# Attention with a mixture of experts on one core: the last bank's copy on VectorE in half of the turns, small gating work on GpSimd

## The chip, the core and the metric

The kernel runs on one core of a Trainium2 chip. A core has TensorE (in profile rows PE for matmuls and PEld for weight loads), VectorE (DVE), ScalarE (ACT), GpSimd (POOL), SyncE (SP), which issues DMAs, and 16 DMA engines. Matmuls write to PSUM, eight banks of 2 KB on each of 128 partitions; the other data lie in SBUF. The metric is the time of one execution in device microseconds (us).

## The reference

The inputs q, k and v are 8 batches x 8 heads x 576 positions x 64 values, in 32-bit floats. What is computed is attention with a block mask, and then a mixture of experts with a capacity of 80 tokens for each of 8 experts:

```python
scores = scale * np.matmul(q, k.transpose(0, 1, 3, 2))
mask = block_i >= block_j                      # blocks of 64 positions
scores = np.where(mask, scores, -1000000000.0)
scores = scores - np.max(scores, axis=-1, keepdims=True)
attn = np.exp(scores)
attn = attn / (np.sum(attn, axis=-1, keepdims=True) + 1e-09)
x = np.matmul(attn, v)                         # 4608 tokens x 512
logits = x @ w_gate
expert_idx = np.argmax(logits, axis=1)
gate_w = softmax(logits)[np.arange(N), expert_idx]
for e in range(8):                             # the 80 tokens of e with the largest gate_w
    out[tok_idx] = gate_w[tok_idx, None] * (np.maximum(x[tok_idx] @ w1[e], 0.0) @ w2[e])
```

## The kernel before, in words

**Pairs and turns.** A batch's eight heads are four pairs; pair i (0 to 31) belongs to batch i // 4. The loop at L799 runs one turn for each pair. Its order is written out by hand: the lists `TURN` (L40), `FIRST`, `LAST` (L139, the last turn, i = 31) hold steps as (distance, name, arguments), and turn i calls the step for pair i + distance. Every engine works through its own instructions strictly in this order and waits by semaphores.

**What a pair goes through.** `load` and `load_v` fetch q, k and v, five and three turns ahead; SP and GpSimd issue these DMAs. `prep` (L570) turns q (`prep 0`) and k (`prep 1`) on VectorE with one 128x576 transpose each; q is also scaled on GpSimd. `ends` and `scores` (TensorE) make the scores of the block-triangular tiles "08", "12", "34", "56" and "78", named after their blocks, 64 to 512 wide, into banks 2 to 7. `max` (VectorE) reduces a tile to its negated maximum; the tiles of the first and last block row are joined by `merge` (L635). `soft` (L640, ScalarE) takes the exponential of a tile with that maximum as bias, and accumulates its sum; the exponential of "78" needs `merge`. `sum "08"` (L648, VectorE) adds up tile "08". `back` (L653, TensorE) transposes the exponentials into banks A, B and C, two banks each (A0, A1 and so on), which `take` (L712) copies to SBUF: TAKE (L29) gives B0 to VectorE and the other five, and the results V0 and V1, to ScalarE. `values` (L683, TensorE) multiplies with v and needs all six copies. `flip` (VectorE) transposes the pair's result for the store.

**Where a turn stands in the trace.** Pair i's exponentials start at the end of turn i - 1. A "turn" in the tables below is the stretch from the first exponential of pair i to that of pair i + 1; it holds the bank copies of pair i, and so most of what turn i lists.

**The order around the change.** In `TURN`, VectorE has this order: small slots (below), max "56" head 0, copy B0, max "08" head 0, max "56" head 1, `prep 1` of pair i + 2, max "78" head 0, a small slot, max "08" head 1, max "78" head 1, `sum "08"`, `merge`, `prep 0`, the four reductions of "34" and "12", `flip`. ScalarE has: V1, V0, B1, A1, A0, C1, C0, then the ten exponentials.

**Gating in slots.** A batch's small work runs in slots: the step `t` (L769, seven in a turn, six of them ahead of max "56" and the seventh between max "78" head 0 and max "08" head 1; eleven in the last turn), `pe`, `ta`, and inside `values`. `enqueue` (L740) is called behind turn 4, 8, ..., 28, and puts generators into queues. In the queue `small` stand `recip` (L368: five little instructions and a reciprocal on VectorE, then the store on SP) and `products` (L420). In turn 5, 9, ... TensorE makes the batch's logits (`pe`), in turn 6, 10, ... it turns them (`logits2`) into banks 2 and 3, the banks of B; `products` reads them there. For batches 0 to 4 a queue in `slow` follows, in which GpSimd adds the products up in a tree and does part of the choice (`choose`, `index`, `total`, `turn`); for batches 5 to 7 `products` ends with a reduction on VectorE (L429), and `shift`, `first_of` and `weight` (L431 to L457) follow on VectorE in `small`. A slot runs one step of the first queue that has one ready; `HOLD_T` closes a queue until the next turn. Then `turn` on GpSimd spreads the weights, `turn2` on TensorE (inside `values`) sums them, and `placed` (VectorE) copies the result into Wt.

**The end.** Behind the last turn VectorE has, in this order, the flip of pair 30, the six instructions of the last batch's `recip`, and the copies of V1 and of a part of V0 (L826 to L839). The logits of batch 7, the choice of tokens, the fetch of the chosen rows, the experts' weights and the two matmuls of each expert follow.

In turn 1, `constants3` (L305) is issued ahead of the list: VectorE computes `cap` (L310) from `cf`, which GpSimd converts (L309).

Of the kernel before, what the change touches and what calls it, by code (L numbers as in the profile page):

```python
# [13 lines left out]
ALU = mybir.AluOpType  # L14
# [4 lines left out]
P = 128  # L19
BLK = 64  # L20
NT = 5
# [18 lines left out]
TURN = (  # L40
    (LEAD, "load"),
    (1, "begin"),
    (1, "ends"),
    (0, "t"),
    (0, "pe"),
    (0, "t"),
    (0, "t"),
    (0, "t"),
# [43 lines left out]
    (-1, "flip"),  # L92
    (3, "load_v"),
)

AHEAD = (
    (LEAD, "load"),
# [6 lines left out]
FIRST = (  # L104
    (LEAD, "load"),
    (1, "begin"),
    (2, "prep", 0),
    (1, "ends"),
    (1, "scores", "2"),
    (1, "max", "56", 0),  # L110
    (1, "soft", "56", 0),
    (1, "max", "56", 1),
# [26 lines left out]
LAST = (  # L139
    (0, "sum", "08"),  # L140
    (0, "pe"),
    (0, "back", "B"),
    (-1, "take", "V1", "v"),
    (-1, "take", "V0", "v"),
    (0, "back", "A"),
    (0, "take", "B0", "v"),
    (0, "take", "B1", "a"),
# [22 lines left out]
def tile_attn_moe(ctx, tc, q, k, v, w_gate, w1, w2, capacity, out, xs=None, dbg=None):  # L170
    nc = tc.nc
    B, H, S, D = q.shape
    NTOK, DM = out.shape
    E, _, F = w1.shape
    NP = H // 2
# [143 lines left out]
    def weights(n, after=None):  # L319
        for _ in loads(n, after):  # L320
            pass
# [33 lines left out]
    def banks(use, where=BANKS):  # L355
        return [psp[i].tile([P, 512], F32, name=f"bank{i}") for i in where[use]]

    class Batch:
# [7 lines left out]
            self.rs = sm.tile([P, NT, H], F32, name="rs", bufs=2)  # L366

        def recip(self):  # L368
            s_, s8 = self.sums, self.sums8
            yield nc.vector.tensor_tensor(s_[BLK:P, NT - 1], s_[BLK:P, NT - 1], s8[BLK:P], op=ALU.add)  # L370
            yield nc.vector.tensor_copy(s_[BLK:P, 0], s8[0:BLK])
            yield nc.vector.tensor_scalar(self.rs, s_, scalar1=1e-9, scalar2=None, op0=ALU.add)
            for to, of in ((slice(0, BLK), slice(BLK, P)), (slice(BLK, P), slice(0, BLK))):
                yield nc.vector.tensor_scalar(self.rs[to, 1], s_[of, 1], scalar1=1e-9, scalar2=None, op0=ALU.add)
            yield nc.vector.reciprocal(self.rs, self.rs)

        def flip(self, pr):

# [41 lines left out]
        def products(self):  # L420
            for pr in range(NP):
                iv = self.la[pr // 2][:, 0:BLK * NT].rearrange("p (t r c) -> p t r c", t=NT, r=2)[:, :, pr % 2, 0:2 * E]
                yield nc.vector.tensor_tensor(
                    prod[:, :, 2 * pr:2 * pr + 2], iv.rearrange("p t (s e) -> p t s e", s=2),
                    self.rs[:, :, 2 * pr:2 * pr + 2].unsqueeze(3).broadcast_to([P, NT, 2, E]), op=ALU.mult)
            if self.b < B - 3:
                return
            self.lg = sm.tile([P, NT, E], F32, name="lg", bufs=2)
            yield nc.vector.tensor_reduce(self.lg, prod.rearrange("p t h e -> p t e h"), axis=AX.X, op=ALU.add)  # L429
# [103 lines left out]
    HOLD_T = object()  # L533
# [182 lines left out]
    def warm(n, wt, after=None):  # L716

        if not n:
            return
        with ExitStack() as order:  # L720
            if after is not None:
                order.enter_context(tc.issue_after(after.ins))
            for i in range(n):
                nc.tensor.matmul(wt.rearrange("p (a c) -> p a c", c=P), lhsT=identr,
                                 rhs=identr.unsqueeze(1).broadcast_to([P, 4, P]), start=(i == 0), stop=(i == n - 1))

    n = B * NP
# [7 lines left out]
    wg_v = w_gate.rearrange("(r s d) e -> s d r e", s=2, d=D)  # L735
    cleared, kept = 0, 2

    pe_, small, slow, acts, turns, issued, held = [], [], [], [], [], {None}, []

    def enqueue(bt):  # L740

        def mark(tag):
            return lambda: issued.add((bt, tag))

        def fill(f, need=None, then=(), to=small):
            to.append((f(), need and (bt, need), then))

        pe_.extend(([bt.logits], [bt.logits2, mark("l2")]))
        turn_ = (lambda: bt.turn(nc.gpsimd), lambda: turns.append((bt, mark("t2"))))
        fill(bt.recip, None, (bt.store,))  # L750
        fill(bt.products, "l2", (mark("pr"),))
        if bt.b < B - 3:
            slow.append([])
            fill(bt.choose, "pr", (mark("sub"),), slow[-1])
            fill(bt.index, None, (), slow[-1])
            fill(bt.total, "ge", turn_, slow[-1])
            fill(bt.placed, "t2", (), slow[-1])
        else:
            fill(bt.shift, None, (mark("sub"),))
            fill(bt.first_of)  # L760
            fill(bt.weight, "ge", turn_)
            fill(bt.placed, "t2")
        acts.append((bt.expo, (bt, "sub"), mark("ge")))
# [3 lines left out]
            f()  # L767

    def t():  # L769
        for of in (small, *slow):  # L770
            while of and not any(of is x for x in held):
                g_, need, then = of[0]
                if need not in issued:
                    break
                step = next(g_, None)
                if step is HOLD_T:
                    held.append(of)
                if step is not None:
                    return
                of.pop(0)  # L780
                for f in then:
                    f()
# [13 lines left out]
    with tc.manual_schedule():  # L796
        warm(WARM[0], banks("g")[0])
        early = loads(FW0)
        for i in range(-LEAD, n):  # L799
            held.clear()  # L800
            if i == -1:
                nc.sync.dma_start(ci, capacity.bitcast(U32).partition_broadcast(P))
                for h in range(2):
                    nc.sync.dma_start(wgd[h * D:(h + 1) * D, :, h * E:(h + 1) * E], wg_v[h])

            for _ in range(min(4, nz - kept - cleared) if i >= n - 5 else 0):
                clear(cleared, nc.sync)
                cleared += 1
            if i == 1 - LEAD:
                nc.scalar.activation(early_exp, ramp[:, 2, 0:1], AF.Exp)  # L810
                constants()
            if i == -1:
                constants2()
            if i == 1:
                constants3()
            if i >= 2 and i % 3:
                next(early, None)
            for d, what, *args in FIRST if i == -1 else AHEAD if i == -2 else TURN if i < n - 1 else LAST:
                if what in slots_:
                    slots_[what]()  # L820
                elif 0 <= i + d < n and not (what == "flip" and n - NP <= i + d < n - 2):
                    getattr(pairs[i + d], what)(*args)
            if n - NP <= i + valued < n - 2:
                pairs[i + valued].flip()
            if i >= flipped and (i - flipped) % NP == NP - 1 and i - flipped < n - 1:
                enqueue(batches[(i - flipped) // NP])  # L826
        for _ in early:
            pass
        while not turns:
            t()  # L830
        bt = batches[B - 1]
        pairs[n - 2].flip()
        for _ in bt.recip():
            pass
        bt.store_sums()
        to, from_ = pairs[n - 1].out.pop("V0")
        pairs[n - 1].take("V1", "v")
        nc.scalar.copy(to[:, 0], from_[:, 0])
        nc.vector.tensor_copy(to[:, 1], from_[:, 1])  # L839
        att.close()  # L840
        fwa = late.enter_context(tc.tile_pool(name="fwa", bufs=FWA, **right, **tw))
        wpools += [fwa] * FWA
        lt = bt.logits_of()
        pairs[n - 1].flip()
        bt.store_x()
        weights(1)
        bt.logits_out(lt)
        bt.logits2()
        bt_, mark = turns.pop(0)
        bt_.turn2(banks("av")[0])  # L850
        mark()
        for _ in (*bt.products(), *bt.shift()):
            pass
        bt.expo()
        while small:
            t()
        found, weighed = bt.first_of(), bt.weight()
        for g_ in (found, found, found, weighed, found, weighed, weighed):
            next(g_)
        bt.turn(nc.vector, 2)  # L860
        bt.turn2(banks("L")[0])
        for _ in bt.placed():
            pass
# [92 lines left out]
    for i in range(NH):  # L956
        junk = sel2.tile([P, 2 * HC], BF16, name="junk", bufs=2)
        counted = vec.tensor_scalar(junk, pall[0][:, 0:2 * HC], scalar1=key[:, 0, i:i + 1], scalar2=None, op0=ALU.is_gt,
                          op1=ALU.add, accum_out=cnt_v[:, i:i + 1])
# [236 lines left out]
    with tc.If(again > 0):  # L1196
# [24 lines left out]
        step = 1.0  # L1221
# [32 lines left out]
        for i in range(2):  # L1254
# [4 lines left out]
                                   op0=ALU.mult, op1=ALU.add)  # L1259
# [29 lines left out]
        more = nc.values_load(nmore_i[0:1, 0:1], min_val=0, max_val=NPASS)  # L1289
# [93 lines left out]
```

## Time and profile before

| | us |
|---|---|
| median of 3 runs (lowest, highest) | 396.56 (396.32, 397.46) |
| the profiled execution | 393.76 |
| its span, first to last instruction | 392.0 |
| TensorE busy | 372.4 |
| ScalarE busy | 290.0 |
| VectorE busy | 279.8 |
| GpSimd busy | 185.4 |

The attention part takes the first 276 us or so of the span, the experts the rest. Times in rows are microseconds from the start of the span, unless marked ns. Busy times are unions over an engine's instructions; instructions of one engine overlap a little, so that the next can start before the one in front has ended. Matmuls are pipelined and their ends are modelled, so a TensorE that is always busy may still be waiting. In a timeline row stand start, length, engine, line, operation, what is written and read, and the count; in square brackets the idle time in front and what ended it.

### The profile page before, as it was taken

How to read it: one execution, taken by the hardware profiler on the slowest of the kernel's cores; microseconds unless marked ns; L12 is line 12 of the kernel's file. 1: busy time of each engine (PE TensorE's matmuls, PEld its weight loads, DVE VectorE, ACT ScalarE, POOL GpSimd, SP SyncE). 2: the span in 40 equal slices, each digit the busy share in tenths (PEclk: the TensorE clock that was granted, in tenths of full speed). 3: DMA queues.
4: the chain of work that ended last, by engine and by line, in shares of the span. 5: the costliest groups of instructions: out<-in, count | busy, mean ns of one | idle time of the engine just before them, and what ended most of it. 6: DMA issues, size and time to landing. Idle time of an engine off the chain costs nothing. (4 is left out here: it accounts for less than half of the span.)

```text
span 392.0 us, 15147 instructions
## 1 busy us (share of the span) xinstructions
PE 372.4 (95%) x5963; PEld 252.9 (65%) x5963; DVE 279.8 (71%) x787; ACT 290.0 (74%) x886; POOL 185.4 (47%) x383
## 2 busy tenths in 40 slices
PE   5899999999999999999999999998899899999991
PEld 3666667666766766766676676676578755665541
DVE  5879899999999989999999999899754230100010
ACT  1799999999999999999999999998122122323231
POOL 6246675566956867666696646500047010000010
PEclk9999999999999999999999999999999899999998
DMA  9989999999999999999999998998677999999801
GB/s 126 153 129 184 144 178 174 178 214 124 181 232 196 154 157 197 162 177 198 131 166 227 153 139 181 328 406 282 160 239 236 367 395 397 394 397 396 301 18 39
DMA packets 169916, 84.39 MB, mean 215 GB/s; under 512 B 132573, under 2 KB 151869, under 8 KB 169840
## 3 DMA queue, kind: packets, MB, share of 16 engines
q1 hardware_dynamic: 158352, 61.80, 74.5%
q0 software_dynamic: 9120, 21.27, 23.8%
q8 instruction: 49, 0.80, 1.0%
q10 hardware_dynamic: 2368, 0.30, 0.6%
q14 instruction: 27, 0.22, 0.2%
HBM read 63.21 MB, written 20.33 MB: 213 GB/s over the span
## 5 line engine op out<-in xcount | busy, mean ns | idle before, releaser
L644 ACT ACTIVATE P<-bank,negm 128x512 f32<-128x512 f32 (+3 forms) x320 | 158.2, 582 | 9.2 <-DVE negm L633 6.5
L597 PE MATMUL bank<-T,qt 64*128 64x320 f32 (+3 forms) x512 | 99.6, 498 | 0.6 <-DVE PT L714 0.6
L633 DVE TENSOR_REDUCE negm<-bank 128x1 f32<-128x320 f32 (+2 forms) x192 | 83.7, 474 | 11.0 <-PE bank L623 11.0
L696 PE MATMUL bank<-PT,vn 128*64 128x64 f32 (+3 forms) x1280 | 88.1, 293 | 0.6 <-ACT PT L714 0.6
L714 ACT COPY PT<-bank 128x512 f32<-128x512 f32 x158 | 81.8, 649 | 2.7 <-PE bank L678 2.2
L696 PEld LDWEIGHTS bank<-PT,vn 128*64 128x64 f32 x1280 | 56.3, 137 | 27.1 <-ACT PT L714 5.2
L580 POOL TENSOR_SCALAR qt<-T 128x128 f32<-128x128 f32 (+2 forms) x96 | 31.3, 344 | 87.5 <-DVE T L573 87.4
L644 ACT ACTIVATION_READ_ACCUMULATOR P<-bank,negm 128x1 f32 x256 | 70.0, 274 | 0.0
L678 PEld LDWEIGHTS bank<-ident,P 64*128 64x128 f32 (+1 forms) x1600 | 58.7, 137 | 12.2 <-issue 6.7
L678 PE MATMUL bank<-ident,P 64*128 64x64 f32 (+1 forms) x1600 | 64.5, 226 | 1.4 <-ACT P L644 0.6
L597 PEld LDWEIGHTS bank<-T,qt 64*128 64x128 f32 x512 | 48.1, 188 | 26.5 <-ACT PT L714 15.2
L633 DVE TENSOR_REDUCE raw<-bank 128x1 f32<-128x64 f32 (+1 forms) x128 | 51.7, 443 | 2.8 <-PE bank L597 1.9
L573 DVE STREAM_TRANSPOSE T<-ld 128x576 f32<-128x576 f32 x64 | 49.3, 771 | 2.7 <-DMA ld<-in_q_dram 1.5
L566 POOL DMA_DIRECT2D vn<-in_v_dram x58 | 46.0, 796 | 1.2 <-PE bank L702 0.8
L1164 POOL DMA_INDIRECT out_dram<-y,si x8 | 7.4, 928 | 74.3 <-DVE y L1159 74.3
L1102 PE MATMUL ps<-xsT,w 128*64 128x80 f32 x1024 | 39.9, 238 | 2.2 <-issue 1.7
L1159 DVE SCALAR_TENSOR_TENSOR y<-av,comb,yt 80x512 f32<-80x512 f32 (+1 forms) x8 | 5.6, 696 | 50.7 <-ACT yt L1158 49.9
L1102 PEld LDWEIGHTS ps<-xsT,w 128*64 128x64 f32 x1024 | 37.8, 140 | 5.8 <-issue 4.5
L558 POOL DMA_DIRECT2D ld<-in_k_dram x54 | 37.3, 697 | 3.8 <-DMA ld<-in_q_dram 3.5
L1155 PE MATMUL av<-w,hT 128*32 128x512 f32 (+2 forms) x320 | 39.0, 553 | 0.0
L1125 ACT ACTIVATE hT<-ps 128x320 f32<-128x320 f32 x16 | 7.0, 438 | 32.0 <-PE ps L1102 32.0
L1158 ACT ACTIVATE yt<-ps,gfar 32x512 f32<-32x512 f32 (+2 forms) x18 | 11.4, 636 | 24.7 <-PE ps L1155 24.6
(190 smaller groups left out, 436.5 us busy)
## 6 DMA issues: line engine op xcount, KB each, us to landing
w<-in_moe_w_dram SPq DMA_DIRECT2D x13, 2048.0 KB, 21.9
xs<-Y SPq DMA_DIRECT2D x32, 288.0 KB, 5.9
out_dram<-zero SPq DMA_DIRECT2D x18, 512.0 KB, 7.2
ld<-in_q_dram SPq DMA_DIRECT2D x126, 72.0 KB, 5.4
vn<-in_v_dram POOLq DMA_DIRECT2D x58, 128.0 KB, 5.1
ld<-in_k_dram SPq DMA_DIRECT2D x72, 72.0 KB, 5.3
w<-in_moe_w_dram POOLq DMA_DIRECT2D x8, 512.0 KB, 7.4
ld<-in_k_dram POOLq DMA_DIRECT2D x54, 72.0 KB, 6.3
```

Of the source, the lines that this page charges most:

```text
L558: eng.dma_start(self.nat[x][r], (q, k)[x][b, h0 + h, :, 32 * i:32 * i + 32] .rearrange("(g r) d -> r g d", r=32))
L566: eng.dma_start(self.vn[:, h], v[b, h0 + h, 0:512].rearrange("(j p) d -> p j d", p=P))
L573: nc.vector.transpose(t, self.nat[x].rearrange("p g d -> p (g d)"))
L580: nc.gpsimd.tensor_scalar(qb[:, to], tb[:, of], scalar1=SCALE, scalar2=1.0, op0=ALU.mult, op1=ALU.mult)
L597: nc.tensor.matmul(s[h][:, c:c + n], lhsT=q_[:, P * t - BLK:P * t + BLK], rhs=k_[:, 0:n], start=(c == 0 and g != "2"), stop=(g == "1"))
L633: nc.vector.tensor_reduce(to[:, b, h:h + 1], self.s[g][h][:, c:c + n], axis=AX.X, op=ALU.max, negate=True)
L644: nc.scalar.activation(Pt[self.i % 2][u][:, h, c1:c1 + n], self.s[g][h][:, c:c + n], AF.Exp, bias=self.negm[:, t, h:h + 1], scale=1.0, acc ...
L678: nc.tensor.transpose(pt[c][0:cols.stop - cols.start, n_ * BLK:(n_ + 1) * BLK], row[u][r, h, cols], ident[r, r])
L696: nc.tensor.matmul(a4[r] if c0 is None else av[r, BLK * c0:BLK * (c0 + b1 - b0)], lhsT=self.vn[:, h, j, :], rhs=self.PT[:, h, row, b0:b1]. ...
L714: (nc.scalar.copy if (eng or TAKE[x]) == "a" else nc.vector.tensor_copy)(*self.out.pop(x))
L1102: yield nc.tensor.matmul(dst(b)[64 * c:64 * (c + 1)], lhsT=w_[:, a, col:col + 64], rhs=x_[:, a], start=(a == 0), stop=(a == n - 1))
L1155: last = nc.tensor.matmul(to[col:col + s1 - s0, c0:c1], lhsT=hT[:, a, s0:s1], rhs=w_[:, a, c0:c1], start=(a == ends[0]), stop=(a == ends[1 ...
```

## The change

In 15 of the 31 turns (1 to 5, and then 8, 9, 12, 13, 16, 17, 20, 21, 24, 25) a second list, `SHARED`, is used. It differs from `TURN` in three steps: `prep 1` stands ahead of the first small slot; C0 is copied by VectorE, right behind the place of C1's copy and so ahead of max "78" head 0; `sum "08"` stands behind `merge`.

The five instructions ahead of the reciprocal run on GpSimd for batches 0 to 6, in one slot, and `HOLD_T` follows, so that the reciprocal comes in the next turn's first slot that `small` gets, and the store behind it. Batch 5 takes the path with the tree on GpSimd. In turns 30 and 31 and behind them the slots serve the `slow` queues first.

Worked through the slots, the reciprocals of batches 0 to 4 come to stand in the first slot of turn 6, 10, ..., ahead of `products`. For the end this gives: in turn 30 the reciprocal and the products of batch 6 ahead of max "56", and its L429 reduction in the seventh slot, where a short reduction stood; in turn 31, batch 5's reciprocal of the sum, and two steps of batch 6, ahead of the last bank copies on VectorE, and behind these `placed` of batch 5, the four steps of `first_of` and the three of `weight`, where the last one of `first_of` and the three of `weight` stood. Batch 5's `turn2` stands ahead of the last `values`.

```diff
+SHARED = list(TURN)
+for step in ((2, "prep", 1), (0, "take", "C0"), (0, "sum", "08")):
+    SHARED.remove(step)
+SHARED.insert(SHARED.index((0, "t")), (2, "prep", 1))
+SHARED.insert(SHARED.index((0, "take", "C1")) + 1, (0, "take", "C0", "v"))
+SHARED.insert(SHARED.index((1, "merge")) + 1, (0, "sum", "08"))
+SHARED = tuple(SHARED)
...
         def recip(self):
+            if self.b < B - 1:
+                self.total_sums(nc.gpsimd)
+                yield HOLD_T
+            else:
+                self.total_sums(nc.vector)
+            yield nc.vector.reciprocal(self.rs, self.rs)
+
+        def total_sums(self, eng):
             s_, s8 = self.sums, self.sums8
-            yield nc.vector.tensor_tensor(s_[BLK:P, NT - 1], s_[BLK:P, NT - 1], s8[BLK:P], op=ALU.add)
-            yield nc.vector.tensor_copy(s_[BLK:P, 0], s8[0:BLK])
-            yield nc.vector.tensor_scalar(self.rs, s_, scalar1=1e-9, scalar2=None, op0=ALU.add)
+            more = {} if eng is nc.vector else dict(scalar2=0.0, op1=ALU.add)
+            more = more or dict(scalar2=None)
+            eng.tensor_tensor(s_[BLK:P, NT - 1], s_[BLK:P, NT - 1], s8[BLK:P], op=ALU.add)
+            eng.tensor_copy(s_[BLK:P, 0], s8[0:BLK])
+            eng.tensor_scalar(self.rs, s_, scalar1=1e-9, op0=ALU.add, **more)
             for to, of in ((slice(0, BLK), slice(BLK, P)), (slice(BLK, P), slice(0, BLK))):
-                yield nc.vector.tensor_scalar(self.rs[to, 1], s_[of, 1], scalar1=1e-9, scalar2=None, op0=ALU.add)
-            yield nc.vector.reciprocal(self.rs, self.rs)
+                eng.tensor_scalar(self.rs[to, 1], s_[of, 1], scalar1=1e-9, op0=ALU.add, **more)
...
-            if self.b < B - 3:
+            if self.b < B - 2:
                 return
             self.lg = sm.tile([P, NT, E], F32, name="lg", bufs=2)
...
-        if bt.b < B - 3:
+        if bt.b < B - 2:
             slow.append([])
...
     def t():
-        for of in (small, *slow):
+        for of in (*slow, small) if len(seen) > n - 2 else (small, *slow):
...
             held.clear()
+            if i >= 0:
+                seen.append(i)
...
-            for d, what, *args in FIRST if i == -1 else AHEAD if i == -2 else TURN if i < n - 1 else LAST:
+            shared = 0 < i < NP or i % NP < 2 and 0 < i < n - NP - 2
+            for d, what, *args in FIRST if i == -1 else AHEAD if i == -2 else LAST if i == n - 1 else SHARED if shared else TURN:
```

## Rows read from the trace of the kernel before

**Rows 1.** The page: busy us of each engine, share of the span, instructions
```profile
PE 372.4 (95%) x5963; PEld 252.9 (65%) x5963; DVE 279.8 (71%) x787; ACT 290.0 (74%) x886; POOL 185.4 (47%) x383
```

**Rows 2.** Windows, turns 11 to 14: length; PE PEld DVE ACT POOL busy; clock
```profile
101.41:109.24 7.83, 7.83 (x146) 5.41 (x144) 7.25 (x20) 7.83 (x26) 6.93 (x16) 1.00 1.27 174
109.24:117.01 7.77, 7.77 (x130) 5.32 (x128) 7.25 (x19) 7.77 (x27) 4.52 (x8) 1.00 1.13 246
117.01:126.02 9.01, 9.01 (x146) 6.03 (x144) 8.39 (x23) 8.76 (x29) 5.90 (x13) 1.00 1.05 205
126.02:134.04 8.02, 8.02 (x140) 5.72 (x138) 7.71 (x22) 7.95 (x26) 5.88 (x11) 1.00 1.08 155
```

**Rows 3.** Timeline of ScalarE at the end of turn 12
```profile
114.62 2.62 ACT L714 COPY PT<-bank 128x512 f32<-128x512 f32 x5
117.01 0.78 ACT L644 ACTIVATE P<-bank,negm 128x448 f32<-128x448 f32 x1
...
118.36 0.83 ACT L644 ACTIVATE P<-bank,negm 128x512 f32<-128x512 f32 x1
```

**Rows 4.** Timeline of VectorE, turn 12
```profile
113.79 0.63 DVE L633 TENSOR_REDUCE negm<-bank 128x1 f32<-128x448 f32 x1 [0.39 <-PE bank L623]
114.33 0.68 DVE L714 COPY PT<-bank 128x512 f32<-128x512 f32 x1
...
115.59 0.77 DVE L573 STREAM_TRANSPOSE T<-ld 128x576 f32<-128x576 f32 x1
116.46 1.42 DVE L633 TENSOR_REDUCE raw<-bank 128x1 f32<-128x512 f32 x3
117.80 0.28 DVE L650 TENSOR_REDUCE sums<-P 128x2 f32<-128x128 f32 x1
118.00 0.21 DVE L637 SCALAR_TENSOR_TENSOR negm<-raw,lower 128x4 f32<-128x4 f32 x1
```

**Rows 5.** Timeline of TensorE, turns 12 and 13: first value product, first B transpose
```profile
109.60 2.75 PE L696 MATMUL bank<-PT,vn 128*64 128x320 f32 x40
...
113.59 1.97 PE L678 MATMUL bank<-ident,P 64*128 64x64 f32 x48
...
117.44 2.75 PE L696 MATMUL bank<-PT,vn 128*64 128x320 f32 x40
...
122.67 1.86 PE L678 MATMUL bank<-ident,P 64*128 64x64 f32 x48
```

**Rows 6.** Timeline of VectorE, turns 13 and 14: sums, reciprocal, products
```profile
120.89 0.17 DVE L370 TENSOR_TENSOR sums<-sums,sums 64x8 f32<-64x8 f32 x1
...
122.02 0.40 DVE L375 RECIPROCAL rs<-rs 128x40 f32<-128x40 f32 x1
...
130.04 0.68 DVE L423 TENSOR_TENSOR prod<-bank,rs 128x80 f32<-128x80 f32 x4
```

**Rows 7.** Timeline of VectorE, turn 1
```profile
25.09 0.16 DVE L310 SCALAR_TENSOR_TENSOR cap<-cf 128x1 f32<-128x1 f32 x1 [1.99 <-POOL cf L309]
```

**Rows 8.** Timeline of TensorE, turn 1
```profile
26.62 1.67 PE L597 MATMUL bank<-T,qt 64*128 64x512 f32 x8 [0.57 <-DVE PT L714]
```

**Rows 9.** Timeline of VectorE, turn 26
```profile
229.35 0.75 DVE L429 TENSOR_REDUCE lg<-prod 128x40 f32<-128x320 f32 x1
```

**Rows 10.** Timeline of ScalarE behind turn 26's merge
```profile
234.40 0.69 ACT L644 ACTIVATE P<-bank,negm 128x512 f32<-128x512 f32 x1 [0.20 <-DVE negm L637]
```

**Rows 11.** Timeline of VectorE, turn 30 and the end of attention
```profile
262.83 0.76 DVE L429 TENSOR_REDUCE lg<-prod 128x40 f32<-128x320 f32 x1
...
273.16 0.19 DVE L449 TENSOR_TENSOR eq<-iota_v,ix 128x40 f32<-128x40 f32 x1
...
273.83 0.77 DVE L379 STREAM_TRANSPOSE Y<-xT 128x576 f32<-128x576 f32 x1
...
276.13 0.22 DVE L714 COPY xT<-bank 128x64 f32<-128x64 f32 x1
```

**Rows 12.** Timeline of TensorE: the last product of the last turn
```profile
275.86 0.22 PE L702 MATMUL bank<-PT,vt 64*64 64x64 f32 x1
```

More of the change, by code (lines that the diff above doesn't have):

```diff
@@ L736, in tile_attn_moe @@
     cleared, kept = 0, 2
-    pe_, small, slow, acts, turns, issued, held = [], [], [], [], [], {None}, []
+    pe_, small, slow, acts, turns, issued, held, seen = [], [], [], [], [], {None}, [], []
     def enqueue(bt):
```

## Prediction

> **What bounds the kernel now.** I read the page first, then the windows of four turns, then the timelines of three engines through them, and last the start and the end of the attention part. On the page ScalarE is busy 290.0 us, VectorE 279.8 and TensorE 372.4 of 392.0 [rows 1]; that averages two parts, so a turn has to be looked at. In turns 11 and 12 ScalarE is busy for the whole of the turn (7.83 of 7.83, 7.77 of 7.77), and VectorE for 7.25 of either. In turn 13, which makes a batch's logits, ScalarE has 0.25 idle (8.76 of 9.01) and VectorE 0.62; in turn 14 they are busy 7.95 and 7.71 of 8.02 [rows 2]. So ScalarE's queue sets an ordinary turn, VectorE has half a microsecond in it, and in turn 13 something else takes part.
>
> ScalarE copies five banks in a row from 114.62 to 117.01, 0.478 each; the last of them is C0, and behind it come the exponentials. The third, of tile 78 and 512 wide, starts at 118.36 [rows 3]. On VectorE the reduction for it starts at 116.46, then the sum of tile 08 at 117.80, then the merge at 118.00, done at 118.21: this exponential follows the merge almost at once [rows 4]. So ScalarE and VectorE are late together there, and a shorter ScalarE queue alone gains nothing.
>
> TensorE's order is values, scores 2, transposes of bank B. From the first value product to the first B transpose it takes 3.99 us in turn 12 (109.60 to 113.59) and 5.23 in turn 13 (117.44 to 122.67) [rows 5]. The logits and their copies stand in between, so turn 13 is set by TensorE with ScalarE.
>
> **(a) The shared turns from 4 on: 4 and 5, 8 and 9, up to 24 and 25; six pairs.** C0 leaves ScalarE: 0.478 less in each turn. On VectorE it is 0.68 long, the next instruction starting 0.60 after it, as behind the B0 copy at 114.33 [rows 4]; it takes the place of the K transpose (0.77 long, about 0.69 from start to start by the same overlap). That transpose now stands first in the turn, where VectorE had 0.39 idle ahead of the reduction at 113.79 [rows 4]: this reduction and the B0 copy start 0.30 later. Then 115.59 + 0.30 + 0.60 = 116.49, against 116.46 for the wide reduction: nearly nothing is lost. The sum now follows the merge: 0.20 earlier. The exponential of tile 78 comes 0.17 earlier, and not 0.478; ScalarE waits for the rest.
>
> That lead enters the second turn of the pair, which TensorE sets. Bank B's transposes there wait for ScalarE's copies of the logits, so part of the lead counts: between 0 and the 0.25 that ScalarE idles there [rows 2]; I take 0.15, with 0.05 for the value products that no longer wait for C0. The second shared turn's own lead meets turn 14. There the products read banks 2 and 3 ahead of bank B's transposes, and the reciprocal (0.40 at 122.02) now stands in front of the products that start at 130.04 [rows 6]. VectorE arrives some 0.3 earlier, so about 0.10 is lost, between 0 and 0.15. Net gain 0.10 a pair (gain of 0.35 to loss of 0.15): **-0.6** (-2.1 to +0.9).
>
> VectorE: DVE Perf Modes in the Trainium skill (section The TRN2 errata) gives a copy out of PSUM 120 + FD cycles at 0.96 GHz on VectorE and 172 + FD at 1.2 GHz on ScalarE: for 512 an estimate of 658 and 570 ns, 88 ns against the move, where the trace has 122 ns from start to start. By the page the 15 copies cost 1.3 us more than they free, by the rows 1.8; the sum above goes by the rows.
>
> **(b) Turns 1 to 3.** In turn 1 VectorE waits 1.99 us for GpSimd ahead of `cap` [rows 7], and TensorE then waits 0.57 for VectorE's B0 copy [rows 8]. The K transpose now stands between that wait and the copy: 0.69 - 0.09 (the copy is shorter) - 0.20 (sum) = +0.40. Turns 2 and 3 gain as the first of a pair does, with no logits behind them: 0.15 each, 0 to 0.478. **+0.1** (-0.55 to +0.5).
>
> **(c) The sums for the reciprocals.** They run on VectorE from 120.89 to 122.02, 1.13 us a batch for seven batches [rows 6]. That turn is TensorE's, so their leaving is worth nothing; without TensorE's chain it would be worth up to 1.13 each. GpSimd is busy 5.90 of 9.01 there [rows 2], and behind the five instructions wait loads for pairs three and five turns ahead. The store goes out one turn later on SP, and it is read only after the attention part. **0**.
>
> **(d) Batch 5's gating.** A reduction of 0.75 (229.35) leaves VectorE in turn 26 [rows 9], where ScalarE then waited 0.20 for the merge [rows 10]; the reciprocal comes in. I take that 0.20 and 0.1 for a short reduction that leaves the merge's path: **-0.3** (-0.55 to 0).
>
> **(e) The end.** Batch 5 now uses slots that were batch 6's. In turn 30 the wide reduction (0.76 at 262.83) moves from ahead of scores 2's reduction to ahead of the merge, and the reciprocal (0.40) takes its old place: +0.35 (0 to 0.65). In the last turn VectorE runs without idle from 273.16 to the V1 copy at 276.13 [rows 11], and V1 is ready when TensorE ends at 276.08 [rows 12]: no slack. Behind the last bank copy come four instructions more (`placed` of batch 5, three of `first_of`): four took 0.67 there (273.16 to 273.83), and `placed` waits for a TensorE product that waits for GpSimd, which no row shows and which I put at 0.2, between 0 and 0.5. That is +0.9 (0.5 to 1.2). Everything that follows (logits, choice, fetch, weights) hangs on V1: **+1.25** (0.5 to 1.85).
>
> **Sum:** -0.6 + 0.1 + 0 - 0.3 + 1.25 = **+0.45 us**, against the profiled execution's 393.76 (span 392.0 and 1.8 around it). It ran 2.8 us under the median of the runs, 396.56; I add the difference to the median: **397.0 us**. A measurement of this kernel tells about 0.3%, 1.2 us, from no change.
>
> **The rivals.**
> *ScalarE alone sets the turns.* It is never idle in turns 11 and 12 [rows 2]. Then 15 copies of 0.478 are worth 7.2, less 1.25 at the end: 390.6 us. Against it: the exponential that follows the merge at once [rows 3, 4], and TensorE's 5.23 [rows 5].
> *The lead goes through.* Copies of the logits are early enough, the reciprocal hides: 0.35 a pair, and turns 1 to 3 at their best: -2.1 - 0.55 - 0.3 + 1.25 = -1.7, so 394.9. For it: both idle times in turn 13 [rows 2]; against it: the products in turn 14.
> *VectorE becomes the bound of the first shared turn*, which is slower. It is busy 7.25 of 7.77 in turn 12 [rows 2]; with 0.60 that is 7.85, and with the 0.10 of idle that the waits for TensorE leave, 7.95: +0.18 in six turns, +1.1, and with (b) to (e) +2.15: 398.7. Against it is the idle that the moved transpose fills [rows 4]. It decides from +0.02 a pair on, since (b) to (e) come to +1.05.
> The Trainium skill's Perfetto Trace Analysis (Optimizing Scalar/DVE Operations) says that with VectorE saturated work may better go to ScalarE, the opposite of this move; by that rule this rival wins, and VectorE's 7.25 of 7.77 half agrees.
>
> **How the numbers follow.** The forecast, inside 1.2 us of no change, has 0.48. ScalarE alone has 0.05 and the lead that goes through 0.19: faster 0.24. VectorE as the bound, with the end as in (e), has 0.28: slower. The range reaches to both middle rivals, 394.5 to 398.8; it leaves out the first rival and about 0.15 at the edges of the other two.
>
> **What would show it.** Right: ScalarE, gapless before, idles ahead of the tile-78 exponential in shared turns; turn 12 stays within 0.2 of 7.77 and turn 13 gets at most 0.25 shorter; turn 1 is longer by some 0.4; in the last turn V1's copy on VectorE starts near 0.9 us after TensorE's last value product ended. Wrong: pairs of shared turns shorter by 0.5 or more, or a V1 copy that starts with TensorE's end.

## The result, and the profile after

The changed kernel takes 403.27 us (median of 6 runs, 400.65 to 404.77) where the kernel before takes 397.01 in the same comparison (6 runs, 396.09 to 400.44). The ratio is 1.0135, interval 1.010 to 1.017: 4.0 to 6.7 us slower. Executions more than 1.5% above the fastest of their kernel are left out of the ratios and spreads below. The forecast was 397.0, at most 398.8. The profiled execution took 401.97, its span 400.2 (before: 393.76 and 392.0).

Engine totals hardly help: of the page after, this is the first part.

```profile
PE 374.8 (94%) x5963; PEld 253.1 (63%) x5963; DVE 279.2 (70%) x762; ACT 285.5 (71%) x871; POOL 196.2 (49%) x428
```

ScalarE has 4.5 less than in [rows 1] and VectorE 0.6 less; the span has 8.2 more. So first the windows of turns 11 to 14, the counterpart of [rows 2]: length, then for PE, PEld, DVE, ACT and POOL the busy time with its instructions, then clock, DMA share and GB/s.

```profile
101.59:109.37 7.78, 7.78 (x130) 5.34 (x128) 6.97 (x17) 7.78 (x27) 5.74 (x11) 1.00 1.30 169
109.37:116.77 7.40, 7.40 (x142) 5.13 (x140) 7.37 (x21) 7.40 (x25) 6.20 (x14) 1.00 1.22 211
116.77:125.50 8.73, 8.73 (x145) 5.71 (x144) 7.92 (x20) 8.36 (x27) 5.91 (x14) 1.00 1.03 217
125.50:134.31 8.81, 8.72 (x143) 6.10 (x141) 8.36 (x22) 8.20 (x27) 6.42 (x16) 1.00 1.09 164
```

Against [rows 2] turn 12 is 0.37 shorter, turn 13 0.28, and turn 14 0.79 longer. Four turns take 32.72 us, before 32.63. The attention part isn't what got slower: turn 31's exponentials start at 265.51, before at 266.11.

The loss lies behind that. VectorE's timeline in the last turn, after (start, duration, engine and line, operation, tiles; in brackets idle time before it and its releaser):

```profile
271.33 1.38 DVE L732 COPY PT<-bank 128x512 f32<-128x512 f32 x2
275.69 0.23 DVE L539 COPY Wt<-bank 128x40 f32<-128x40 f32 x1 [2.98 <-PE bank L720]
275.81 0.19 DVE L463 TENSOR_TENSOR eq<-lg,mx 128x40 f32<-128x40 f32 x1
...
277.18 0.77 DVE L397 STREAM_TRANSPOSE Y<-xT 128x576 f32<-128x576 f32 x1
...
279.06 0.40 DVE L383 RECIPROCAL rs<-rs 128x40 f32<-128x40 f32 x1
279.38 0.16 DVE L732 COPY xT<-bank 128x64 f32<-128x64 f32 x1
```

TensorE's timeline there, after:

```profile
272.27 0.35 PE L533 MATMUL bank<-sp,sameR 128*32 128x40 f32 x16 [0.30 <-POOL sp L524]
272.61 2.75 PE L714 MATMUL bank<-PT,vn 128*64 128x320 f32 x40
...
275.42 0.22 PE L719 MATMUL bank<-PT,vn 64*64 64x64 f32 x1
275.42 0.22 PE L720 MATMUL bank<-PT,vt 64*64 64x64 f32 x1
279.69 2.15 PE L421 MATMUL bank<-xT,wgd 128*32 128x288 f32 x16 [4.05 <-DVE xT L732]
```

The copy at L539 is `placed` of batch 5. The 16 products that it reads (L533) end at 272.6; it starts at 275.69, released by the last value products. (The profile names L720; in the kernel's text it is L719, beside it at 275.42, that writes the bank of the 16 products.) Behind it on VectorE stand the choice and the weights of batch 6, a transpose of outputs, and the sums and reciprocal of batch 7, so V1 is copied at 279.38, 3.74 us after TensorE's last value product ended (275.64). Before it was 0.05 us after it [rows 11, 12]. TensorE idles 4.05 us, and its granted clock falls. The windows from 274 on, after and then before:

```profile
274.00:278.00 4.00, 1.64 (x28) 0.95 (x24) 2.12 (x10) 0.37 (x1) 0.56 (x1) 0.99 0.33 81
278.00:282.00 4.00, 2.31 (x17) 0.87 (x17) 2.51 (x9) 0.51 (x2) 0.23 (x1) 0.50 0.14 22
282.00:286.00 4.00, 3.79 (x32) 2.97 (x32) 2.75 (x14) 0.53 (x2) 0.00 (x0) 0.50 0.82 190
286.00:290.00 4.00, 4.00 (x28) 2.92 (x28) 1.70 (x9) 0.00 (x0) 0.10 (x1) 0.73 0.89 221
```

```profile
274.00:278.00 4.00, 3.67 (x55) 1.85 (x51) 3.41 (x10) 0.96 (x3) 1.00 (x2) 1.00 0.67 157
278.00:282.00 4.00, 3.77 (x38) 2.79 (x37) 3.02 (x15) 0.45 (x2) 0.00 (x0) 1.00 0.64 143
282.00:286.00 4.00, 3.44 (x35) 2.71 (x35) 3.16 (x18) 0.13 (x1) 1.48 (x7) 1.00 0.86 196
286.00:290.00 4.00, 3.35 (x22) 2.43 (x20) 3.28 (x18) 2.40 (x12) 1.36 (x6) 1.00 0.99 366
```

After, 0.50 (1.2 GHz) holds from 278 until some time in 286 to 290; before, it is 1.00 (2.4 GHz) throughout. The rows that measure what both do to the end are the first gather of the tokens on GpSimd, before and after:

```profile
291.74 1.14 POOL L993 DMA_INDIRECT xg<-xs,gi  x1 [4.21 <-ACT occ L1040]
```

```profile
297.06 1.14 POOL L1014 DMA_INDIRECT xg<-xs,gi  x1 [3.64 <-DVE gi L1004]
```

From the start of turn 31's exponentials to the gather: 291.74 - 266.11 = 25.63 before, 297.06 - 265.51 = 31.55 after. That is 5.92 more, less the 0.60 by which turn 31 came earlier: 5.3, which is what the ratio says (1.35% of 397 is 5.4). The rest of the 8.2 between these two profiled executions comes after the gather, and is not shown to be part of the change (last section).

### The profile page after: what moved, and what is told of

Same layout as the page of the kernel before. It is cut to its first block, busy times and chain, and to the rows that moved or that the text cites. A ratio compares the mean times of both kernels' runs of the same rounds, so it can differ in the third digit from the quotient of the medians.

```text
span 400.2 us, 15188 instructions
## 1 busy us (share of the span) xinstructions
PE 374.8 (94%) x5963; PEld 253.1 (63%) x5963; DVE 279.2 (70%) x762; ACT 285.5 (71%) x871; POOL 196.2 (49%) x428
## 5 line engine op out<-in xcount | busy, mean ns | idle before, releaser
L732 ACT COPY PT<-bank 128x512 f32<-128x512 f32 x143 | 74.4, 643 | 5.0 <-PE bank L696 4.9
L662 ACT ACTIVATION_READ_ACCUMULATOR P<-bank,negm 128x1 f32 x256 | 63.5, 248 | 0.0
L1123 PE MATMUL ps<-xsT,w 128*64 128x80 f32 x1024 | 40.7, 238 | 3.1 <-issue 3.1
L732 DVE COPY PT<-bank 128x512 f32<-128x512 f32 x49 | 33.5, 683 | 1.8 <-PE bank L696 1.6
```

The lines of the kernel that those rows point to most:

```text
L662: nc.scalar.activation(Pt[self.i % 2][u][:, h, c1:c1 + n], self.s[g][h][:, c:c + n], AF.Exp, bias=self.negm[:, t, h:h + 1], scale=1.0, acc ...
L732: (nc.scalar.copy if (eng or TAKE[x]) == "a" else nc.vector.tensor_copy)(*self.out.pop(x))
L1123: yield nc.tensor.matmul(dst(b)[64 * c:64 * (c + 1)], lhsT=w_[:, a, col:col + 64], rhs=x_[:, a], start=(a == 0), stop=(a == n - 1))
```

## The experiments

Theory: the copy of batch 5's turned weights waits for the value products, which are summed in the same PSUM bank (3 us); the idle time that follows costs TensorE its clock (as much again). Rivals: the added VectorE steps are too many; another part of the change; the weights' stream. Each ratio is to the kernel before on the same chip (its median was 394.2 to 397.5 in the three comparisons). The times that the expectations name go by its 397.0 of the first comparison, so they are compared as ratios.

**A bank of its own.**

```diff
-                bt.turn2(self.last[:, 5 * BLK:])
+                own = self.i == n - 1
+                bt.turn2(banks("B", self.where)[0] if own else self.last[:, 5 * BLK:])
```

> The changed kernel, but in the last turn the product that turns batch 5's weights gets a PSUM bank of its own (the one that bank B0's copy left free) instead of columns of the bank in which the last value products are summed. Theory 'shared bank': the copy of batch 5's turned weights waits on VectorE for the last value product, because both write the same bank, and eight VectorE steps, the K transpose, the sums and the reciprocal of batch 7 stand behind it; with a bank of its own the copy starts within 0.3 us of its product (near 272.7), V1's copy starts 0 to 0.9 us after TensorE's last value product instead of 3.7, TensorE's granted clock stays 1.00 from 274 to 290, and the time is 395.5 to 398.0. Rival 'chain too long': the added VectorE steps themselves make V1 late; then V1's copy still starts over 2 us after the last value product and the time is 401 or more. Rival 'the stream': the late weight loads are slower for another reason; then V1 is early and the time is still over 400.

Ratio 0.9988 (0.9957 to 1.0019): the whole loss is gone. VectorE's timeline there:

```profile
272.65 0.23 DVE L539 COPY Wt<-bank 128x40 f32<-128x40 f32 x1
272.77 0.19 DVE L463 TENSOR_TENSOR eq<-lg,mx 128x40 f32<-128x40 f32 x1
...
274.15 0.77 DVE L397 STREAM_TRANSPOSE Y<-xT 128x576 f32<-128x576 f32 x1
...
276.07 0.40 DVE L383 RECIPROCAL rs<-rs 128x40 f32<-128x40 f32 x1
276.39 0.16 DVE L733 COPY xT<-bank 128x64 f32<-128x64 f32 x1
```

The same steps in the same order (the transpose among them is that of outputs; my text calls it K's), and the copy starts at 272.65 with no wait. V1 follows 0.81 us behind the last value product (275.58). The clock is 1.00 in every window to 290. The chain of steps was not too long: the shared bank is shown as the cause of the loss.

**TensorE kept busy, the wait left in.**

```diff
+        warm(17, banks("B", LAST_BANKS)[1])
         lt = bt.logits_of()
```

> The changed kernel with 17 matmuls more (512 columns, result unused, into a free bank) between the last value product and the last batch's logits, in the 4.3 us in which TensorE stood idle; VectorE's wait stays. Theory 'wait and then clock': V1's copy still starts 3.7 us after the last value product, but the granted clock stays 1.00 from 276 to 290 where it was 0.50, the logits take 1.35 us instead of 2.08 and the first row of dummy matmuls 3.5 instead of 5.1, so the gathering of the tokens starts some 3 us after the kernel before and not 6; time 399 to 401. Rival 'wait alone': the clock costs nothing that ends last; time 402.5 to 404.5. Rival 'the clock alone': time 396 to 398.

Ratio 1.0070 (1.0037 to 1.0104), between the two. Its windows:

```profile
274.00:278.00 4.00, 4.00 (x53) 2.83 (x52) 0.96 (x6) 0.37 (x1) 0.00 (x0) 1.00 0.00 0
278.00:282.00 4.00, 4.00 (x30) 2.60 (x28) 3.70 (x13) 0.27 (x1) 0.81 (x1) 1.00 0.06 4
282.00:286.00 4.00, 3.76 (x41) 2.92 (x38) 2.68 (x14) 0.77 (x3) 0.00 (x0) 1.00 0.62 138
286.00:290.00 4.00, 3.45 (x33) 2.33 (x31) 3.36 (x20) 0.00 (x0) 1.19 (x5) 1.00 0.84 190
```

VectorE still waits 2.98 us for L720, but the clock stays up. The gather starts 28.75 us after turn 31's exponentials: the wait is worth 28.75 - 25.63 = 3.1, the clock 31.55 - 28.75 = 2.8. So matmuls whose result nobody uses make the changed kernel faster. The ratios say it less clearly (1.0070 against 1.0135, intervals that touch) than the gather's rows.

The rows also show where the clock's 2.8 arises. The logits, the twelve unused matmuls behind them (L742, L743) and VectorE's copy of the last batch's weights, whose product stands behind those on TensorE; the changed kernel, and then the one with the own bank:

```profile
279.69 2.15 PE L421 MATMUL bank<-xT,wgd 128*32 128x288 f32 x16 [4.05 <-DVE xT L732]
283.49 5.17 PE L742 MATMUL ps<-identr 128*128 128x512 f32 x12
289.01 0.23 DVE L539 COPY Wt<-bank 128x40 f32<-128x40 f32 x1 [2.09 <-PE bank L533]
```

```profile
276.60 1.18 PE L421 MATMUL bank<-xT,wgd 128*32 128x288 f32 x16 [1.02 <-DVE xT L733]
279.03 3.01 PE L743 MATMUL ps<-identr 128*128 128x512 f32 x12
283.09 0.23 DVE L539 COPY Wt<-bank 128x40 f32<-128x40 f32 x1 [0.40 <-PE bank L533]
```

From V1's copy (279.38 and 276.39) to this copy it is 9.63 us and 6.70: the difference is 2.9, so the whole price of the clock lies here. Half of it (1.5) comes ahead of the unused matmuls and half from their start on. The unused matmuls that the kernel has there take 2.2 us longer at the low clock, and useful work stands behind them.

**The parts of the change one by one.** First the shared order alone, put into the kernel before:

> The kernel before with the shared turns alone (order of the turn and the C0 copy on VectorE), sums and gating as before. My forecast for these parts was -0.6 and +0.1, so 396.5 (from -2.65 to +1.4: 394.4 to 398.4). By the two traces, where four turns from one that is not shared to the next take 32.6 to 32.8 us in both, it is 396.0 to 397.8, with turns 12 and 13 shorter by 0.3 to 0.4 each and turn 14 longer by 0.7 to 0.8. Rival 'ScalarE alone': 390. Rival 'the order of the turn also does harm at the end': 400 or more.

1.0011 (0.9973 to 1.0049): no measurable difference. Turns 12 and 14 are 0.49 shorter and 1.56 longer in its profile, turn 13 0.23 longer instead of shorter. In turn 13 a K load came late for the transpose that now stands first in the turn (VectorE's timeline), a price that the new order can have and that I had not named:

```profile
124.34 0.78 DVE L582 STREAM_TRANSPOSE T<-ld 128x576 f32<-128x576 f32 x1 [1.12 <-DMA ld<-in_k_dram]
```

Then the change without batch 5's gating:

```diff
-            if self.b < B - 2:
+            if self.b < B - 3:
...
-        for of in (*slow, small) if len(seen) > n - 2 else (small, *slow):
+        for of in (small, *slow):
```

> The changed kernel without batch 5's gating on GpSimd (its slots in their old order; the reciprocal sums on GpSimd for batches 0 to 4 alone, those of 5 and 6 on VectorE as before). Theory 'shared bank': batch 5's turned weights are copied in an earlier turn, V1's copy follows the last value product within 0.2 us, the clock stays up, time 395.5 to 398. Rival 'another part': the shared turns or the sums on GpSimd bring the loss; time over 400.

0.9973 (0.9948 to 0.9998): as expected, and a little faster than the kernel before. The last of these, the sums alone:

> The kernel before with the sums for the reciprocals of batches 0 to 4 on GpSimd, nothing else. Forecast: nothing, ratio 0.998 to 1.002, since the turn in which they lie is set by TensorE. Rival 'VectorE sets that turn': 1.13 for each of five batches, 5.6 us faster, ratio 0.986. Rival 'GpSimd is late': K loads and scaled queries come later, ratio over 1.004.

0.9964 (0.9937 to 0.9991), 0.4 to 2.5 us faster, and not the nothing that I forecast. Its ten executions lie between 392.7 and 393.8, those of the kernel before beside it between 392.5 and 398.1. So the shortest are alike, and what the sums take away is long executions. The other four kernels on that chip that have the sums moved and no late V1 stay below 395.7 too; the two without the sums (the shared order alone, and turn 1 alone below) reach 398.6 and 397.7. Which stretch makes those long is not shown, since one execution of each was profiled.

**Turn 1, and the shared turns on top of the cure.** Both kernels here have the bank of their own:

```diff
-            shared = 0 < i < NP or i % NP < 2 and 0 < i < n - NP - 2
+            shared = i % NP < 2 and NP <= i < n - NP - 2
```

> The changed kernel with a bank of its own for batch 5's turned weights (as in the run before), and turns 1 to 3 in the old order; the pairs from 4 on stay shared. Theory 'a long wait in turn 1': the moved K transpose of turn 1 waits for GpSimd ahead of B0's copy, TensorE stands idle for 1.4 to 2.0 us instead of 0.57, and in some executions its granted clock is then 0.50 for 3 to 4 us, which makes turn 2 1.3 longer; without it turn 1 takes 7.7 to 7.8, the clock stays 1.00 from 26 to 34, and the ratio to the kernel before is 0.992 to 0.998, 0.5 to 2 us below the run with the bank alone (0.9988). Rival 'taken up later': the ratio is that run's within 0.001.

0.9964 (0.9937 to 0.9990), inside the range expected, but the reason is not shown: the profile of this kernel, with turn 1 in the old order, has the low clock too (28 to 32):

```profile
28.00:32.00 4.00, 4.00 (x34) 2.38 (x32) 4.00 (x11) 2.53 (x10) 0.90 (x3) 0.57 1.06 159
```

Here turn 2 takes 10.60 us, where before takes 8.78. With `shared = False`:

> As the kernel with turns 1 to 3 in the old order, but with no shared turn at all: C0 stays on ScalarE everywhere. What is left of the change is the sums and the gating on GpSimd, with the bank of its own. Theory 'given back': the 0.27 that each of two shared turns gains from values to values on TensorE is lost in the next two turns, so this kernel's time is that of the one with the shared pairs within 0.5 us (0.0013), with 32.5 to 32.8 us for four turns. Rival 'the forecast': 0.6 slower than with the pairs. Rival 'ScalarE alone': 5 us slower.

0.9959 (0.9931 to 0.9988). Without any shared turn the time is the same within the intervals: the copies on VectorE in the 12 turns from 4 on bring nothing that can be measured. Turn 1 alone, in the kernel before:

> The kernel before with turn 1 alone in the shared order. My forecast was +0.40 there. Theory 'a long wait in turn 1': TensorE's idle time ahead of the scores grows from 0.57 to 1.4 to 2.0, turn 1 gets 0.35 to 0.9 longer, and where the clock falls turn 2 gets 1.3 longer as well: ratio to the kernel before 1.001 to 1.005. Rival 'taken up later': ratio 0.999 to 1.001.

1.0011 (0.9976 to 1.0046): undecided by time. By the profiles, turn 1 takes 8.06 to 9.28 us in the seven that share it, and 7.69 to 7.71 in six of the seven that don't (8.38 in the kernel with turns 1 to 3 in the old order). The low clock behind it came in four of the former and one of the latter.

**The same wait by other means.** The changed kernel itself, beside the next three:

> The changed kernel itself once more, beside the next three. Theory 'wait and then clock': the granted clock falls to 0.50 behind the last value product in this execution too, the gathering of the tokens starts some 6 us after the kernel before measured from turn 31, ratio 1.010 to 1.017. Rival 'one unlucky execution': the clock stays up and the ratio is 1.006 to 1.009, the wait alone.

1.0117 (1.0043 to 1.0190), with the same 2.98 us ahead of the copy and the clock at 0.50 from 278.5 on. The gather comes 31.71 us after turn 31's exponentials, in the first profile 31.55. Then, in the kernel before, one transpose done five times:

```diff
-        pairs[n - 2].flip()
+        for _ in range(5):
+            pairs[n - 2].flip()
```

> The kernel before with nothing of the change, but four more transposes on VectorE (the same one repeated, some 0.74 each, 3.0 in all) ahead of V1's copy in the last turn. Theory 'wait and then clock': any 3 us there leaves TensorE idle for some 3.3 us, the granted clock falls to 0.50 behind it, and the time grows by 5 to 7 us: ratio 1.012 to 1.018. Rival 'wait alone': 3 us, ratio 1.007 to 1.009. Rival 'what hangs on V1 is hidden by the weights': ratio under 1.004.

1.0100 (1.0020 to 1.0180), less than I expected, and the interval holds the rival's 1.008 too. TensorE idled 3.32 us, and the clock fell for a shorter time:

```profile
278.00:282.00 4.00, 1.17 (x16) 0.41 (x16) 3.70 (x11) 0.39 (x1) 0.00 (x0) 1.00 0.15 26
282.00:286.00 4.00, 3.75 (x33) 2.93 (x33) 2.60 (x14) 0.65 (x3) 0.00 (x0) 0.57 0.63 139
286.00:290.00 4.00, 3.94 (x33) 2.72 (x32) 2.73 (x15) 0.00 (x0) 0.76 (x3) 1.00 0.91 198
```

The same with 13 unused matmuls in the gap:

> The same four transposes, and 13 matmuls whose result is unused on TensorE in that time. Theory 'wait and then clock': the clock stays 1.00 from 274 to 300 and the time grows by the wait alone, 2.5 to 3.5 us: ratio 1.006 to 1.009, some 0.006 under the kernel without the matmuls. Rival 'wait alone': the same ratio as without them.

1.0087 (1.0043 to 1.0131). The gather came 29.22 us after turn 31's exponentials without them, 28.40 with them (25.63 before): the wait 2.8, the clock 0.8. By time the two are not told apart, so this 0.8 rests on one profile of each. "Any 3 us there" holds for the wait. What the clock adds differs between the two ways to wait: the changed kernel has the low clock for some 10 us in both of its profiles, and the kernel with the repeated transpose for 3.4.

**The sums in one slot, but on VectorE.**

> The kernel before with the sums of batches 0 to 4 in one slot and the reciprocal and the store a turn later, as the change has them, but still on VectorE. The kernel with them on GpSimd had 0.9964 [0.9937, 0.9991]. Theory 'the engine': with the sums on VectorE the ratio is 1.000 within 0.002. Rival 'the later store': it is again 0.996 to 0.998.

0.9978 (0.9945 to 1.0011): just inside the rival's range, and the interval holds both theories. Its longest execution took 397.9, that of the kernel before beside it 400.7, so long executions are gone here too; that speaks for the slot and the later store rather than the engine, but doesn't settle which gives the 0.4%.

## Why the prediction was wrong

**The step that failed** is in (e): "`placed` waits for a TensorE product that waits for GpSimd, which no row shows and which I put at 0.2, between 0 and 0.5". The product was done in time. What the copy waited for was the bank: `turn2` writes columns of the tile in which the value products are summed, and the copy, standing behind them in the order of the program, waits for that tile's last writer. It cost 2.98 us and not 0.2. I had looked for the producer of the data, and not for who else writes to the same tile. Before, the same copy stood in the first slot of the next turn or later, when the value products had long ended, so that the wait cost nothing and showed as no idle time; the kernel's text showed it, with `turn2` and the value products both on `self.last`.

The Trainium skill's Perfetto Trace Analysis (Optimizing Tensor Performance, Matmuls) says that independent groups of matmuls should rotate through different PSUM banks, so that the copies out of one overlap the matmuls of the next. The own bank agrees: the copy at 272.65 instead of 275.69.

**The second step that failed** is "Everything that follows (logits, choice, fetch, weights) hangs on V1", by which the end is late by as much as V1 and no more. TensorE's idle time of 4.05 us had a price of its own, the clock, here 2.8 us. The kernel before already has unused matmuls ahead of products that would wait (12 of them take 3.02 us from 279.00 on), and its last turn had 0.33 of idle there. The clock was in no term of the sum.

By the other terms:
- **(a)** forecast -0.6; 0.9964 with the shared pairs and 0.9959 without, so no gain is measured, though intervals of some 1 us to either side don't exclude one of 0.6. That ScalarE would idle ahead of the tile-78 exponential was right (0.12); here ScalarE, after:

```profile
118.13 0.20 ACT L662 ACTIVATION_READ_ACCUMULATOR P<-bank,negm 128x1 f32 x1
118.45 0.69 ACT L662 ACTIVATE P<-bank,negm 128x512 f32<-128x512 f32 x1
```

  It waits for VectorE's merge (118.13 to 118.35), and not for ScalarE's own work [rows 3, 4]. The size was wrong: from the first exponential of the stretch to this one it is 9.08 us, before 9.12 [rows 2, 3], so it comes 0.04 earlier and not 0.17. Turn 12 fell by 0.37, more than the 0.2 that I allowed, and the pair by 0.65, which I had named as a sign that I was wrong. It was no gain all the same, since turn 14 gave it back. There TensorE's order sets the pace, and ScalarE waits for it, after:

```profile
130.70 0.74 ACT L732 COPY xT<-bank 128x64 f32<-128x64 f32 x2
131.92 2.55 ACT L732 COPY PT<-bank 128x512 f32<-128x512 f32 x5 [0.47 <-PE bank L696]
```

  So "about 0.10 is lost" in turn 14 was mis-sized: all of the lead is lost. Pair 13's value products start at 126.36, before at 126.41, although the exponentials ahead of them start 0.52 earlier.
- **(b)** forecast +0.1 with +0.40 in turn 1: turn 1 got 0.35 longer in the changed kernel's profile, 0.5 to 1.6 in the others that share it. Turns 2 and 3, forecast 0.15 shorter each, take 8.79 and 7.71, before 8.78 and 7.76. The mechanism in turn 1 was right; TensorE now idles 1.46 us ahead of the scores, where [rows 8] has 0.57:

```profile
26.94 1.40 PE L615 MATMUL bank<-T,qt 64*128 64x512 f32 x6 [1.46 <-DVE PT L732]
```

- **(c)** forecast 0; by the runs -1.4 (-2.5 to -0.4). Why is open: turns 11 to 14 don't get shorter by it, and the shortest executions don't either.
- **(d)** forecast -0.3: the wait of 0.20 [rows 10] is gone, after:

```profile
234.02 0.70 ACT L662 ACTIVATE P<-bank,negm 128x512 f32<-128x512 f32 x1
```

  The stretch that holds it, from the first exponential of pair 27 on, takes 7.75 to 7.78 us in all six profiles with batch 5's gating as changed and 8.25 to 8.27 in the eight without it: 0.5 shorter, more than forecast. Whether it lasts is not shown: turns 26 to 30 take 41.50 before and 40.77 in the changed kernel, but over all profiles 40.7 to 42.2 with that gating and 40.9 to 42.2 without.
- **(e)** without the bank's wait: turn 30 takes 8.22, before 8.27, so the +0.35 was wrong; V1 comes 0.81 behind TensorE, where I had 0.9 with 0.2 for a wait in it, so that was near. And yet only 0.04 reaches the gather (last section).

The rivals all lay elsewhere: none had a wait of VectorE for TensorE in the last turn. ScalarE alone didn't set the turns (no 7 us), and the lead didn't go through.

## What to carry to other kernels

When a copy moves ahead in a queue, look up every writer of the tile that it reads, not only the writer of its data: two results that share a PSUM bank can be ready only together, with the later of them, as here. Ask of every new idle time of TensorE whether its clock stays up behind it, and try unused matmuls there where it doesn't. Look also at what unused matmuls stand ahead of, since at the low clock they hold it up. And judge a lead over the whole period of the loop: what two turns gain, the third may take back.

## What the runs showed beyond that

The clock can fall twice. In some executions TensorE's granted clock is low again among the first matmuls of the experts, while the DMA engines are busy throughout, the kernel before included (the first fence), and a kernel whose end is that of before (the sums in one slot, the second):

```profile
308.00:312.00 4.00, 2.50 (x41) 2.31 (x41) 1.41 (x10) 1.19 (x4) 0.00 (x0) 0.81 1.02 413
312.00:316.00 4.00, 4.00 (x66) 3.07 (x67) 2.38 (x14) 0.44 (x1) 0.00 (x0) 0.76 1.02 397
```

```profile
300.00:304.00 4.00, 2.35 (x22) 1.52 (x21) 0.00 (x0) 0.00 (x0) 3.23 (x10) 0.65 1.03 353
304.00:308.00 4.00, 4.00 (x55) 3.66 (x53) 0.89 (x4) 0.86 (x2) 0.00 (x0) 0.50 1.04 335
```

From the gather to the end of the span it is 100.3 us in the first and 104.0 in the second; other profiles have 99.7 to 104.4, and the changed kernel 103.1. So 3 us of the 8.2 between the two profiled executions come from there. They go with the chip and the execution: of the twelve experiments, the four on one chip all have this second fall in their profiles, whatever the kernel, and two of the eight on the other. That the change has no part in it is not shown, since all five profiles with a late V1 have it. On that other chip alone the kernel before ran from 392.3 to 398.1.

The later V1 didn't count. With the own bank the logits start 0.83 later after turn 31's exponentials than before, and the gather 0.04 later. Its row:

```profile
291.14 1.14 POOL L1015 DMA_INDIRECT xg<-xs,gi  x1 [3.64 <-DVE gi L1005]
```

It follows the indices, ready at 290.86; before, the indices were ready at 290.86 too, but the gather waited for a ScalarE copy as well (`occ`) and started at 291.74. The six profiles of kernels with batch 5's gating as changed have no such wait, the eight without it do. What puts the wait there was not tried.
